# The plain first product in step 2 of a fused pooled-attention and MLP kernel, with the next query transpose and V load issued a step earlier

## The chip, the cores and the metric

One core of a Trainium2 chip runs the whole kernel. The metric is the device time of one execution in microseconds (us). The kernel before takes 282.59 us, the median of three runs (282.27 to 282.88). The profile is one execution with a span of 280.3 us.

## The reference

Two stages are fused. The first is attention over pooled keys and values: 8 batches, 8 heads, 576 queries of 64 elements; keys and values are averaged over groups of 8 rows, so each query sees 72 of them. The second is a two-layer MLP with a tanh GELU on the 4608 tokens.

```python
# q, k, v: [8, 8, 576, 64] f32;  w_in: [512, 2048], w_out: [2048, 512] f32
k_p = k.reshape(B, H, Sp, 8, D).mean(axis=3)       # Sp = 72
v_p = v.reshape(B, H, Sp, 8, D).mean(axis=3)
scores = np.matmul(q, k_p.transpose(0, 1, 3, 2)) / np.sqrt(D)
attn = softmax(scores)                             # over the 72 pooled keys
x = np.matmul(attn, v_p)                           # then heads side by side: [4608, 512]
h = x @ w_in                                       # first product
g = gelu_tanh(h)
out = g @ w_out                                    # second product, [4608, 512] f32
```

## The kernel before

The kernel works in nine steps of 512 tokens. Steps 0 to 6 and 8 are the first 512 tokens of one batch each, step 7 the 64 left over from each of the eight. During the MLP of one step, the attention of the next one is prepared: its query transpose, K pooling, K transpose, K spread, V pooling, V spread, scores, exponentials, normalisation, transposes of the weights (eT), and the V product, whose result xT the next MLP reads. Each of these is hung as a hook on a position in the row of matmuls. Positions 0 to 63 are the first product, 64 to 175 the second; a hook only says where in each engine's order an instruction stands.

The first product has two forms. The plain one has 64 matmuls of 512 columns; its outputs lie in a ring of four PSUM banks ("mm"):

```python
def hidden_two(g, hook):
    hp = [psum.tile([128, MAIN], F32, name="mm", tag="mm", bufs=4) for _ in range(2)]
    for s, (f, ko) in enumerate([(0, 0), (0, 1), (1, 0), (1, 1), (0, 2), (0, 3), (1, 2), (1, 3)]):
        hook(s)
        nc.tensor.matmul(out=hp[f], lhsT=w_in_b[:, ko, f * 128:(f + 1) * 128], rhs=st[g]["xT"][:, ko, :],
                         start=(ko == 0), stop=(ko == 3))
    for f in range(2):
        nc.scalar.activation(out=gT[:, f, :], in_=hp[f], func=ACT.Gelu_apprx_tanh)
# then 14 times hidden(): 4 matmuls of 512 columns and a GELU
```

The split one replaces half of the first product by seven products of half-sized blocks in place of eight, with sums ahead of them and additions behind, on VectorE and ScalarE. It starts in the two-bank tiles ("sc") that also hold the scores:

```python
def hidden_fast(g, hook, rest):
    y, x = [psum.tile([128, 2, MAIN], F32, name="c2", tag="sc", bufs=2) for _ in range(2)]
    # ...
    product(x4, 1, A(0, 0), X(0, 0), 0)        # 8 matmuls of 256 columns
    rest()                                     # values(g, 1): half 1 of the V product
    (t1, t2, t3, t4), make = x_sums(g)         # four VectorE sums of xT
    make(1, 2)
    k2, k0, k1 = part(), part(), spare
    nc.scalar.copy(out=k2, in_=x4)
    product(y4, 1, A(1, 0), X(1, 0), 4)
    add(out=k2, in0=y4, in1=k2, op=ALU.add)    # VectorE
    make(3, 4)
    hidden(g, 0, hook, 8)
    hidden(g, 1, hook, 12)
    product(x4, 0, S(2), T(t2), 16)
    nc.scalar.copy(out=k0, in_=x4)
    gelu(0, 0, k2)
    product(y4, 1, S(1), T(t1), 20)
    nc.vector.tensor_copy(out=k1, in_=y4)
    # ... three more products, two more additions, six more hidden()
```

The second product is split in all of the steps from 1 on. Its accumulators y, x and z are three banks of the ring of four:

```python
for n, (prod, acc, fresh) in enumerate([(1, xs, 1), (2, y, 1), (6, xs, 0), (5, z, 1), (7, xs, 0), (3, z, 0), (4, xs, 0)]):
    # 16 matmuls of 256 columns each, at positions 64 + 16 * n ...
    # after 1 and 6: ScalarE copies x out; after 5: ScalarE copies z, VectorE adds y;
    # after 7: VectorE adds x; after 3: VectorE adds z, first store;
    # after 4: ScalarE copies x, second store
```

It reads sums of the GELU's outputs (`g_sums`: per group of rows three sums on VectorE, and a fourth), the second of which overwrites a part of gT in place.

The V product has two halves of 256 tokens. Half 0 goes to an "sc" tile and one ScalarE copy takes it to xT; half 1 goes to two banks of the "mm" ring, and ScalarE and VectorE copy one each:

```python
def values(g, half, split=True):
    # half 0: one tile of tag "sc"; half 1: two tiles of tag "mm"
    # 16 matmuls of 256 columns on parts of the array (line 337)
    if half == 0 or not split:
        copy([nc.scalar, nc.vector][half], xT[:, :, t0:t0 + 256], xo)
    else:
        for i, eng in enumerate((nc.scalar, nc.vector)):
            copy(eng, xT[:, 2 * i:2 * i + 2, t0:t0 + 256], xo[i])
```

The exponentials of a step's four score tiles are ScalarE instructions that write the buffers e, of which there are three; the normalisation of tile 0 on VectorE is the last reader of its e. K and V of a step lie in one of two buffers kv, and all loads, stores and transposes of these steps are issued by one queue (SP).

Of the kernel before, what the change touches and what calls it, by code (L numbers as in the profile page):

```python
# [19 lines left out]
def kernel(  # L20
# [21 lines left out]
    nc = tc.nc  # L42
    B, H, S, D = q.shape
# [278 lines left out]
    def values(g, half, split=True):  # L322

        eT, t0 = st[g]["eT"], 256 * half
        if half == 0 or not split:
            xo = psum.tile([128, HP, 256], F32, name="xo", tag="sc", bufs=2)
            dst = [xo[:, pr, :] for pr in range(HP)]
        else:
            xo = [psum.tile([128, 2, 256], F32, name="xo", tag="mm", bufs=4) for _ in range(2)]
            dst = [xo[pr // 2][:, pr % 2, :] for pr in range(HP)]  # L330
        if g < B:
            for part, rows_ in ((SMALL, 32), (BIG, 64)):
                for pr in range(HP):
                    for hh in range(2):
                        r0, c = part[2 * pr + hh]
                        n = dict(PARTS[pr])[c]
                        nc.tensor.matmul(out=dst[pr][64 * hh:64 * hh + 64],  # L337
                                         lhsT=vbd[r0:r0 + rows_, g, n, 64 * hh:64 * hh + 64],
                                         rhs=eT[r0:r0 + rows_, 2 * half:2 * half + 2, c, :],
                                         start=(part is SMALL and pr % 2 == 0), stop=(part is BIG), skip_group_check=True)  # L340
        else:
            for pr in range(HP):
                for b in range(4):
                    p0 = 64 * (b % 2)
                    for x, (c, n) in enumerate(PARTS[pr]):
                        nc.tensor.matmul(out=dst[pr][:, 64 * b:64 * b + 64], lhsT=vbd[:, 4 * half + b, n, :],
                                         rhs=eT[:, 2 * half + b // 2, c, p0:p0 + 64], start=(x == 0), stop=(x == 1))
        xT = st[g]["xT"]
# [5 lines that stand above are left out]
# [408 lines left out]
    def at(hooks, s, f, *a):  # L762
        hooks.setdefault(s, []).append(lambda: f(*a))
# [7 lines left out]
    hooks = {}  # L771
# [46 lines left out]
    for n_, g in enumerate(seq):  # L818
        if n_ == 0:
            continue  # L820
        hooks = {}
        fast = n_ >= 2
        if n_ == 1:
            for i in range(1, 4):
                at(hooks, i, w_sums, i, 0, NP, nc.vector)
            at(hooks, 36, g_sums, 0, 4)
            at(hooks, 57, g_sums, 4, 6)
        elif fast:
            at(hooks, 41, g_sums, 0, 2, (0,))
            at(hooks, 57, g_sums, 2, 6, (0,))  # L830
            at(hooks, 65, g_sums, 6, 8, (0,))
            at(hooks, 65, g_sums, 0, 8, (1,))
        else:
            at(hooks, 20, g_sums, 0, 2)
            at(hooks, 36, g_sums, 2, 4)
            at(hooks, 57, g_sums, 4, 6)
        if not fast:
            at(hooks, 65, g_sums, 6, 8)
        if n_ + 1 < len(seq):
            n = seq[n_ + 1]  # L840
            b = B - 1 if n == R else n
            kv = n != B - 1
            if n_ == 1:
                for j in range(4):
                    at(hooks, 28 + 4 * j, cast_q, n, j, j + 1, nc.scalar)
                at(hooks, 41, qT_tile, n)
                at(hooks, 41, q_transpose_dma, n)
            if kv and not fast:
                t0 = 22 if n_ == 1 else 12
                at(hooks, t0, pool, b, 0, 5)  # L850
                at(hooks, t0, dup_k, b, 0, 5)
                at(hooks, t0, kT_tile, b, None)
                at(hooks, t0, k_transpose_dma, b)
                t1 = t0 + (16 if n_ == 1 else 24)
                at(hooks, t1, pool, b, 5, 9)
                at(hooks, t1, spread_v, b, nc.gpsimd)
                at(hooks, 56, k_spread, b, [nc.vector, nc.vector])
            elif kv:
                at(hooks, 17, pool, b, 0, 5, (1,))
                at(hooks, 17, dup_k, b, 0, 5)  # L860
                at(hooks, 17, kT_tile, b, None)
                at(hooks, 17, k_transpose_dma, b)
                if n_ == 2:
                    at(hooks, 41, pool, b, 5, 9)
                    at(hooks, 41, spread_v, b, nc.gpsimd)
                else:
                    at(hooks, 17, spread_gated, b)
                at(hooks, 40, k_spread, b, [nc.gpsimd, nc.gpsimd])
            if fast:
                at(hooks, 2, qT_tile, n)  # L870
                at(hooks, 2, q_transpose_dma, n)
                if n_ == 2:
                    at(hooks, 3, load_kv, n, (1,))
                sc_at = [76, 76, 100, 100]
                norm_at = [84, 88, 106, 106]
            else:
                sc_at = [68, 68, 94, 94]
                norm_at = [81, 97, 104, 114]
            for j in range(4):
                at(hooks, sc_at[j], scores, n, j)  # L880
                at(hooks, max(sc_at[j], 80), exps, n, j)
            at(hooks, norm_at[0], eT_tile, n)
            if fast:
                for j in (2, 3):
                    at(hooks, norm_at[j], sums, n, j)
            for j in range(4):
                at(hooks, norm_at[j], norm, n, j, nc.gpsimd if j == 1 else nc.vector)
                at(hooks, norm_at[j], e_transpose_dma, n, j)
            at(hooks, 64 + 66, nc.scalar.preload_act_table_set, GELU_SET)
            at(hooks, 64 + 100, xT_tile, n)  # L890
            at(hooks, 64 + 100, values, n, 0)
        if n_ + 2 < len(seq):
            n2 = seq[n_ + 2]
            s2 = 44 if n_ == 1 else 8 if n2 == R else 57
            at(hooks, s2, q_tile, n2)
            if n2 == R:
                at(hooks, s2, load_q, n2, 0, 2, nc.sync)
                at(hooks, 30, load_q, n2, 2, 4, nc.sync)
            else:
                at(hooks, s2, load_q, n2, 0, 4, nc.sync)  # L900
            at(hooks, 64 + 52, cast_gated, n2)
            if n2 != B - 1:
                b2 = B - 1 if n2 == R else n2
                if n_ >= 2:
                    at(hooks, 64 + 84, pool, b2, 5, 9, (0,))
                    at(hooks, 64 + 97, pool, b2, 5, 9, (1,))
                at(hooks, 64 + 98, pool, b2, 0, 5, (0,))
            if n_ == 1:
                at(hooks, 45, load_kv, n2, (0,))
            else:  # L910
                at(hooks, 28, load_kv, n2)
        mlp(g, hooks, n_ + 1 == len(seq), fast, lambda: values(g, 1))
# [30 lines left out]
```

## Time and profile before

| | |
|---|---|
| time | 282.59 us (282.27 to 282.88) |
| span of the profiled execution | 280.3 us |
| TensorE matmuls | 271.6 us busy, 97% |
| VectorE | 228.4 us busy, 81% |
| ScalarE | 176.9 us busy, 63% |
| GpSimd | 68.0 us busy, 24% |
| DMA | 54.36 MB, mean 194 GB/s |

The profile page has a row for each engine (PE is TensorE, PEld its weight loads, DVE VectorE, ACT ScalarE, POOL GpSimd), a strip of 40 slices, the chain of work that ended last, and the costliest groups of instructions by source line. The trace behind it answers more closely: a timeline (start, length, engine, line, output and inputs, and in brackets the idle time before and what ended it), a list of waits, and busy times within chosen stretches. Lines that come up below: 337 is the V product, 374 and 522 the plain first product, 465 the products of the split one, 577 the second product, 253 the exponentials, 149 to 152 the pooling of K and V, 425 to 429 the sums for the second product, 491 to 508 the copies and additions of the split first product, 449 its sums of xT, 275 the normalisation, 92 and 94 copies by ScalarE and by VectorE or GpSimd.

### The profile page before, as it was taken

What the parts mean: (1) busy time and instruction counts of PE and PEld (TensorE: products, weight loads), DVE (VectorE), ACT (ScalarE), POOL (GpSimd) and SP (SyncE); (2) the same over time, 40 slices, a digit from 0 to 9 for tenths busy, and PEclk for the clock granted to TensorE, in tenths of its full rate; (3) what the DMA queues carried; (4) which work ended last, traced back from release to release, by engine and by line L of the source; (5) the groups of instructions that cost most, each with busy time, mean ns of one, the idle gap of its engine ahead of it and who ended that gap; (6) DMA issues with size and microseconds to landing.
All of it is one profiled execution on the core that took longest, in us unless ns stands there. A gap on an engine that the chain in (4) does not pass through costs nothing.

```text
span 280.3 us, 6585 instructions
## 1 busy us (share of the span) xinstructions
PE 271.6 (97%) x2710; PEld 194.0 (69%) x2710; DVE 228.4 (81%) x370; ACT 176.9 (63%) x256; POOL 68.0 (24%) x105
## 2 busy tenths in 40 slices
PE   8989999999999979999999999999999999999995
PEld 3678844446867667668766876687668966876684
DVE  5886769998969999989998999898989378937832
ACT  1586585487647943786479647964796469646820
POOL 4740263003220634131412142214221300100000
PEclk9999999999999999999999999999999999999999
DMA  7999999999969965688869958995741860163013
GB/s 233 307 194 290 372 386 220 314 315 230 237 199 240 317 202 147 154 272 263 147 163 262 263 145 197 241 247 161 165 150 27 161 137 0 26 144 78 1 40 112
DMA packets 71695, 54.36 MB, mean 194 GB/s; under 512 B 45554, under 2 KB 57842, under 8 KB 71666
## 3 DMA queue, kind: packets, MB, share of 16 engines
q1 hardware_dynamic: 69410, 51.72, 70.3%
q0 software_dynamic: 2112, 2.10, 4.7%
q8 instruction: 21, 0.34, 0.5%
q10 hardware_dynamic: 144, 0.13, 0.1%
q14 instruction: 8, 0.07, 0.1%
HBM read 36.70 MB, written 9.44 MB: 165 GB/s over the span
## 4 chain that ended last, share of the span: by engine, by line
PE 80%; DVE 13%; DMA 3%; issue 1%; ACT 0%; POOL 0%; SPq 0%; DVEq 0%; ACTq 0%; POOLq 0%
PE mm L577 29%; PE mm L374 18%; PE c L465 14%; PE mm L385 5%; PE xo L337 3%; PE x L577 2%; DVE den L260 2%; PE warm L676 2%; PE sc L244 2%; DVE eb L275 2%; DMA qT<-q_b 2%; DMA out_dram<-osb 1%; DVE kv L149 1%; PE mm L390 1%; DVE kv L151 1%
## 5 line engine op out<-in xcount | busy, mean ns | idle before, releaser
L374 PE MATMUL mm<-xT,w_in_b 128*128 128x512 bf16 x280 | 65.2, 379 | 0.0
L577 PEld LDWEIGHTS <-gT 128*128 128x128 bf16 x512 | 48.8, 98 | 9.2 <-issue 1.6
L376 ACT ACTIVATE gT<-mm 128x512 bf16<-128x512 f32 x70 | 40.0, 598 | 12.9 <-PE mm L374 12.6
L374 PEld LDWEIGHTS <-w_in_b 128*128 128x128 bf16 x280 | 27.4, 98 | 27.1
L577 PEld LDWEIGHTS <-stage 128*128 128x128 bf16 x384 | 37.0, 98 | 6.5 <-issue 1.3
L92 ACT CAST xT<-xo 128x512 bf16<-128x512 f32 (+1 forms) x17 | 13.4, 786 | 32.3 <-PE xo L337 27.4
L577 PE MATMUL mm<-tw,gT 128*128 128x256 bf16 x240 | 29.9, 273 | 0.3 <-DVE osb L562 0.3
L577 PE MATMUL mm<-tw,stage 128*128 128x256 bf16 x224 | 28.0, 273 | 1.5 <-ACT osb L92 1.2
L172 POOL TENSOR_TENSOR vbd<-kvb,vmask 128x256 bf16<-128x256 bf16 (+2 forms) x40 | 23.4, 606 | 23.1 <-DVE kvb L152 17.0
L577 PE MATMUL mm<-w_out_b,gT 128*128 128x256 bf16 x240 | 28.9, 273 | 0.0
L260 DVE TENSOR_REDUCE den<-e 128x8 f32<-128x576 f32 x36 | 26.0, 737 | 3.5 <-ACT e L253 3.5
L253 ACT ACTIVATE e<-sc 128x576 f32<-128x576 f32 x36 | 22.6, 654 | 9.6 <-PE sc L244 4.5
L92 ACT COPY osb<-mm 128x512 f32<-128x512 f32 x30 | 17.5, 586 | 16.7 <-PE mm L577 15.6
L465 PEld LDWEIGHTS <-ws 128*128 128x128 bf16 x224 | 21.9, 98 | 7.3 <-issue 0.3
L275 POOL TENSOR_TENSOR eb<-e,r 128x576 bf16<-128x576 f32 x7 | 8.0, 1149 | 70.9 <-DVE r L269 66.1
L94 POOL CAST q_b<-q_sb 128x1024 bf16<-128x1024 f32 (+1 forms) x15 | 19.7, 1337 | 19.3 <-DMA q_sb<-in_q_dram 19.3
L149 DVE TENSOR_TENSOR kv<-kv 128x1024 f32<-128x1024 f32 (+3 forms) x19 | 21.2, 1117 | 3.2 <-DMA kv<-in_k_dram 2.1
L465 PE MATMUL c<-tt,ws 128*128 128x256 bf16 x168 | 20.8, 273 | 0.1
L275 DVE TENSOR_TENSOR eb<-e,r 128x576 bf16<-128x576 f32 x25 | 19.8, 793 | 0.9
L94 DVE CAST xT<-xo 128x512 bf16<-128x512 f32 (+1 forms) x10 | 7.4, 745 | 13.1 <-PE xo L337 7.9
L465 PEld LDWEIGHTS <-w_in_b 128*128 128x128 bf16 x168 | 15.9, 98 | 3.1 <-issue 1.2
L385 PE MATMUL mm<-xT,w_in_b 128*128 128x256 bf16 x128 | 15.6, 273 | 0.1
(105 smaller groups left out, 426.2 us busy)
## 6 DMA issues: line engine op xcount, KB each, us to landing
kv<-in_k_dram SPq DMA_DIRECT2D x7, 1024.0 KB, 7.1
q_sb<-in_q_dram SPq DMA_DIRECT2D x7, 1024.0 KB, 9.9
kv<-in_v_dram SPq DMA_DIRECT2D x6, 1024.0 KB, 8.8
out_dram<-osb SPq DMA_DIRECT2D x12, 512.0 KB, 2.9
out_dram<-osb SPq DMA_DIRECT2D x11, 256.0 KB, 4.0
kv<-in_v_dram SPq DMA_DIRECT2D x4, 512.0 KB, 9.9
w_in_b<-in_moe_w_in_dram POOLq DMA_DIRECT2D x4, 512.0 KB, 6.7
w_out_s<-in_moe_w_out_dram SPq DMA_DIRECT2D x2, 1024.0 KB, 13.5
```

Of the source, the lines that this page charges most:

```text
L92: eng.copy(out=out, in_=in_)
L94: eng.tensor_copy(out=out, in_=in_)
L149: add(out=t[:, :, 0:4, :], in0=t[:, :, 0:4, :], in1=t[:, :, 4:8, :], op=ALU.add)
L172: eng.tensor_tensor(out=vbd[p0:128, b, n0:n1, :].rearrange("p (c r) (hh d) -> p c (r hh) d", c=max(m, 1), d=D), in0=kvb[p0:128, 4 + c0:4 + ...
L253: nc.scalar.activation(out=e.rearrange("p (x h) s -> p x (h s)", x=2), in_=sc[:, :, 0:4 * Sp], func=ACT.Exp, scale=1.0 / 64.0)
L260: nc.vector.reduce_sum(out=den, in_=e, axis=AX.X)
L275: eng.tensor_tensor(out=o.rearrange("p (pr hh s) -> p hh pr s", hh=2, s=Sp), in0=e.rearrange("p (hh pr) s -> p hh pr s", hh=2), in1=r.rear ...
L374: nc.tensor.matmul(out=hp, lhsT=w_in_b[:, ko, fo * 128:(fo + 1) * 128], rhs=st[g]["xT"][:, ko, :], start=(i == 0), stop=(i == KO - 1))
L376: nc.scalar.activation(out=gT[:, fo, :], in_=hp, func=ACT.Gelu_apprx_tanh)
L385: nc.tensor.matmul(out=hp[:, f, :], lhsT=w_in_b[:, ko, (fo + f) * 128:(fo + f + 1) * 128], rhs=st[g]["xT"][:, ko, c0:c0 + 256], start=(ko ...
L465: nc.tensor.matmul(out=acc[:, m, :], lhsT=lhs(i, m), rhs=rhs(i), start=bool(fresh and i == 0 and m % 2 == 0), stop=(i == 1), skip_group_ch ...
L577: nc.tensor.matmul(out=xs[p] if acc is xs else acc[:, p, :], lhsT=lt, rhs=rt, start=bool(fresh and m == 0 and (p == 0 or (last and acc is ...
```

## The change

Step 2 gets the plain first product instead of the split one; the split form stays from step 3 on. With the plain form the hooks of step 2 become those of step 1: the sums for the second product in smaller pieces (positions 20, 36, 57, 65), K pooling for step 3 in one go at 12, V pooling and V spread at 36, K spread on VectorE at 56, scores at 68 and 94, normalisation at 81, 97, 104 and 114. There is no `rest()` in the plain form, so half 1 of step 2's V product moves to the end of step 1 (position 171). Also at the end of step 1, from position 164, stand the transpose of step 3's queries and behind it the load of step 3's V, which were issued at positions 2 and 3 of step 2; the first pass of step 3's K pooling, which stood at 162, moves into step 2. The purpose is to relieve VectorE in step 2, and to have the queries and V of step 3 on their way before it begins.

```diff
@@ for n_, g in enumerate(seq):
-        fast = n_ >= 2
+        fast = n_ >= 3
@@ elif kv:                          # steps with the split form
                 at(hooks, 17, k_transpose_dma, b)
-                if n_ == 2:
-                    at(hooks, 41, pool, b, 5, 9)
-                    at(hooks, 41, spread_v, b, nc.gpsimd)
-                else:
-                    at(hooks, 17, spread_gated, b)
+                at(hooks, 17, spread_gated, b)
                 at(hooks, 40, k_spread, b, [nc.gpsimd, nc.gpsimd])
             if fast:
                 at(hooks, 2, qT_tile, n)
                 at(hooks, 2, q_transpose_dma, n)
-                if n_ == 2:
-                    at(hooks, 3, load_kv, n, (1,))
@@
             at(hooks, 64 + 100, values, n, 0)
+            if n_ < 2:
+                at(hooks, 64 + 107, values, n, 1)
@@
             at(hooks, 64 + 52, cast_gated, n2)
-            if n2 != B - 1:
+            if n_ < 2:
+                at(hooks, 64 + 100, qT_tile, n2)
+                at(hooks, 64 + 100, q_transpose_dma, n2)
+                at(hooks, 64 + 100, load_kv, n2, (1,))
+            elif n2 != B - 1:
                 b2 = B - 1 if n2 == R else n2
-                if n_ >= 2:
-                    at(hooks, 64 + 84, pool, b2, 5, 9, (0,))
-                    at(hooks, 64 + 97, pool, b2, 5, 9, (1,))
+                at(hooks, 64 + 84, pool, b2, 5, 9, (0,))
+                at(hooks, 64 + 97, pool, b2, 5, 9, (1,))
                 at(hooks, 64 + 98, pool, b2, 0, 5, (0,))
```

On TensorE step 2 loses 56 matmuls of 256 columns and gains 32 of 512. VectorE and ScalarE lose the copies, sums and additions of one split first product, and ScalarE has 16 GELUs of 512 elements in place of eight of 512 and four of 1024.

## The prediction

> **What bounds the kernel now.** I read the page's first two blocks first: the PE row (TensorE's matmuls) is busy 97% of the 280.3 us span, the clock row is full throughout. So the whole change can only be worth the few microseconds in which TensorE waits, plus or minus the matmuls that it adds. Then I cut the trace into steps, each from the first V product of one step (line 337) to that of the next. The columns of this view are the stretch, its length, and the busy time and count of each engine; the third row here is step 4, which I take as the undisturbed pattern:
>
> ```profile
> 78.64:108.78 30.14, 28.32 (x297) 20.39 (x296) 26.73 (x41) 18.83 (x26) 8.86 (x12) 1.00 0.83 227
> 108.78:136.72 27.94, 27.94 (x297) 20.46 (x296) 26.02 (x42) 19.24 (x26) 8.57 (x13) 1.00 0.79 209
> 136.72:164.56 27.84, 27.84 (x297) 20.52 (x297) 25.30 (x41) 19.04 (x26) 7.84 (x13) 1.00 0.81 214
> ```
>
> Step 2, the first row, is 30.14 - 27.84 = 2.30 us longer than step 4 with the same matmuls: 1.82 us of idle TensorE (30.14 - 28.32), and 0.48 us that the busy column hides, because matmuls take about 0.16 us to flow again after a wait (twelve products from 99.38 should, at step 4's 1.32 us and with the 0.36 us idle shown below, end at 101.06; the next one starts at 101.23). The timeline of TensorE (start, length, then in brackets the idle before and its releaser) puts this at three places in the second product:
>
> ```profile
> 100.13 1.26 PE L577 MATMUL mm<-tw,stage 128*128 128x256 bf16 x10 [0.36 <-DVE stage L427]
> 104.31 1.91 PE L577 MATMUL mm<-tw,stage 128*128 128x256 bf16 x16 [1.17 <-ACT osb L92]
> 108.26 0.60 PE L577 MATMUL mm<-tw,gT 128*128 128x256 bf16 x4 [0.29 <-DVE osb L562]
> ```
>
> The middle one names ScalarE's copy out of PSUM, yet ScalarE was not busy. Its timeline, and VectorE's, tell why:
>
> ```profile
> 103.14 0.65 ACT L253 ACTIVATE e<-sc 128x576 f32<-128x576 f32 x1 [3.11 <-PE mm L577]
> 103.68 1.07 ACT L92 COPY osb<-mm 128x512 f32<-128x512 f32 x2
> ...
> 92.81 1.44 DVE L149 TENSOR_TENSOR kv<-kv 128x1024 f32<-128x1024 f32 x1
> ...
> 102.26 0.76 DVE L275 TENSOR_TENSOR eb<-e,r 128x576 bf16<-128x576 f32 x1
> ```
>
> The fourth exponential stood at the head of ScalarE's queue for 3.11 us. The bracket names a matmul that had long been done; the true releaser is found in the buffers. It writes one of three e buffers, and the one it needs is freed by VectorE's first normalisation, which ends at 102.26 + 0.76 = 103.02. The copy stands behind it. So all three waits have one cause: **VectorE is late in step 2.** The chain that ended last agrees: from 90.35 to 108.2 us it runs through VectorE almost alone, whereas in steps 3 to 6 it runs through TensorE. VectorE is late because only step 2 has the whole V pooling (92.81 to 95.63, 2.8 us) between the sums of the second product; later steps do it at the end of the step before.
>
> **What the Trainium skill says.** "TensorE: Matmul & The Clock Gate", section "Wait — 56ns, not 53.3ns?", gives for back-to-back matmuls N columns at 2.4 GHz plus about 2.5 ns, 215.7 ns at 512 columns. The trace agrees: 64 products of 512 columns in step 1 run from 52.22 to 66.04, 13.82 us or 215.9 ns each. The same page, under "Architectural detail", calls ScalarE and VectorE strict FIFO; the copy held behind the blocked exponential is that. "GPSIMD Engine Reference", section "1. Specifications", says that GpSimd shares its SBUF interfaces with VectorE where VectorE has two SBUF inputs. The trace agrees: the sum at line 426 takes 1.03 us at 96.27, beside GpSimd's spread of V, and 0.69 us at 60.19 without it.
>
> **The change, part by part.**
>
> 1. *Matmuls.* The split first product has 56 matmuls of 256 columns and 32 of 512. In step 2 it runs from 80.66 to 94.48, 13.82 us, with 16 V products of 0.70 us inside: 13.12. The plain one has 64 of 512, 13.82 as in step 1. So TensorE gets **+0.70 us** of work. The 16 V products are moved into step 1, not removed.
>
> 2. *VectorE.* Gone are three combining additions (1.23, 1.22, 1.23), one copy (1.21) and four sums of x (0.41, 0.42, 0.41, 0.42): 6.55 us. The K spread comes over from GpSimd: two copies, 0.93 us at 64.57 in step 1. Net -5.6 us inside the step. The first K pooling pass (1.48) moves from before the step's start to just after. None of this is on the path by itself; it is what empties the VectorE queue before the second product.
>
> 3. *The start of step 2, a new wait.* The split form starts in the wide score banks and has work while xT is copied. The plain form starts in the four-bank ring. From the last V product of step 1 at 78.64: 0.70 for half 0 of V, 7 of the remaining products 0.77, half 1 of V 0.70 (to 80.81), 5 products, and by 1.32 + 1.40 in sum TensorE is at 81.36; I add 0.1 for a second change of tile shape: 81.45. The first plain product needs xT's second half and a ring bank: the ring holds y, x, z of step 1's output, then the two V accumulators, so the next bank is x, which ScalarE copies out only after step 1's last product. ScalarE: first xT copy 79.47 to 80.48 (as now), second from 80.97 (0.58) to 81.55, copy of x 0.20 behind the last product as now (80.66 to 80.86), so 81.65 to 82.23. With 0.1 us to start, TensorE resumes at 82.33: **+0.88 us** idle that was not there.
>
> 4. *Second product of step 2.* The hooks become those of step 1, whose second product, from 66.04 to 78.64, took 12.60 us with one wait in it, 0.35 us idle plus 0.16, for the query transpose of step 2. In the new step 2 that transpose is issued a step early, so 12.60 - 0.51 = 12.09.
>
> 5. *Sum.* 82.33 + 13.82 + 12.09 = 108.24, against 108.78 now: **-0.54 us**. In other terms: -2.30 of waits, +0.70 plain product, +0.88 start, +0.1 tile change, +0.1 the looser second product. Step 3 is 0.10 longer than step 4 now, half of which may go: -0.6 in all. Steps 4 to 8 are the same instructions. 282.59 - 0.6 = **282.0 us**.
>
> *Is VectorE in time?* Its queue after the xT copy (81.66): K pooling 1.48 + 0.82 + 0.49 + 0.26 to 84.7; first sums when the fourth GELU is out (about 86.5) to 88.2; the next two from about 90.0 to 91.7; V pooling 2.33 (as at 62.25 in step 1) to 94.0; K spread to 95.0; sums 4 to 6 at step 1's slowed 2.3 to 97.3; the last, 1.7, to 99.0. TensorE reads the changed gT of the last pair at 96.15 + 1.75 + 0.39 + 0.66 = 98.95; that operand is the second of four sums, ready near 98.2. Margin 0.75.
>
> **The rivals.**
>
> A. *V lands late and VectorE stands still instead.* V of step 3 is issued behind the query transpose, which holds the issuing queue 3.28 us. Now: issue 85.26, landing 6.6 us later at 91.9. After: the transpose follows the store that issues at 79.03 (0.7), so 79.7 to 83.0, V at 83.0 + 6.6 = 89.6. Needed at 91.7. A V of 9.4 us, as another one in this stretch took, would land at 92.4, and 0.7 late is within the margin. Likely harmless; if not, 282.5 to 283.5.
>
> B. *The start is worse than 0.88.* Half 1 of V needs the last transpose of eT: issued 77.11, landed 2.6 later at 79.71; it is needed at 80.11. Now it has 1.9 us, then 0.4. If it or the copies slip by 0.6, the gain is gone: 282.6.
>
> C. *TensorE simply pays for the extra columns* and step 2's waits remain in part, because score banks and the e buffers still tie ScalarE to VectorE. For it: step 1's x addition ends at 77.71, only 0.4 us ahead of the product that needs it at 78.11. Against it: step 1 shows no such wait. It would make 282.5 to 283.3.
>
> D. *A larger gain*: the copy of x goes earlier, or the early transpose and V unload step 3 too. Down to 281.2.
>
> **Range and chances.** The gain is a difference of 2.30 and about 1.8, each known to perhaps 0.4, and the runs themselves spread by 0.6 us. I put 8 in 10 on 281.1 to 282.9. Two per cent is 5.7 us, more than twice all that is idle in step 2; only a long stall would be slower by so much.
>
> **What would show it.** Right: a wait of 0.8 to 1.0 us at line 522 for ScalarE; no wait over 0.2 us in step 2's second product, and ScalarE's fourth exponential no longer held 3 us; step 2 at about 29.6 us from V product to V product; step 3 at 27.84 to 27.94. Wrong: VectorE idle at the V pooling waiting for the V transfer (A), TensorE waiting at line 337 for eT (B), or the 1.17 us wait for the ScalarE copy still there (C).

## The result, and the profile after

The changed kernel takes 280.73 us (median of four runs, 280.68 to 280.84) against 282.50 for the kernel before: ratio 0.9937, 95% interval 0.9919 to 0.9954. Run once more beside the last experiment it took 281.09 (280.68 to 281.73), ratio 0.9956 (0.9943 to 0.9969). The gain is thus 1.2 to 1.8 us; the prediction had 0.6 and a range that ended at 281.1. The direction and the cause were right, the size was not.

The steps first, from V product to V product: this is the view of busy times in chosen stretches, for the changed kernel (stretch, length, then TensorE, weight loads, VectorE, ScalarE and GpSimd busy; the last three columns are the granted clock, the share of the DMA engines and GB/s).

```profile
78.69:107.68 28.99, 28.98 (x274) 18.26 (x274) 22.68 (x41) 18.34 (x28) 6.28 (x10) 1.00 1.00 240
107.68:135.51 27.83, 27.83 (x297) 20.49 (x297) 25.59 (x42) 19.04 (x26) 8.12 (x13) 1.00 0.80 207
135.51:163.34 27.83, 27.83 (x297) 20.51 (x296) 25.30 (x41) 19.03 (x26) 7.83 (x13) 1.00 0.81 207
```

Step 2 went from 30.14 to 28.99 us, and 28.98 of it is busy by this column. Step 3 is now as short as step 4. What TensorE does at the start of step 2, where a new wait of 0.88 us was foretold, is in its timeline, and beside it ScalarE's:

```profile
80.26 0.77 PE L337 MATMUL xo<-eT,vbd 32*64 32x256 bf16 x16
80.96 0.72 PE L577 MATMUL mm<-tw,gT 128*128 128x256 bf16 x5
81.69 1.89 PE L522 MATMUL mm<-xT,w_in_b 128*128 128x512 bf16 x8
...
81.06 0.58 ACT L92 CAST xT<-xo 128x512 bf16<-128x512 f32 x1 [0.52 <-PE xo L337]
81.72 0.59 ACT L92 COPY osb<-mm 128x512 f32<-128x512 f32 x1
```

No row of TensorE has a bracket. The plain first product (line 522) starts at 81.69, just after the copy of xT ends (81.06 + 0.58), and before ScalarE has even begun to copy x out (81.72). So it does not lie in x's bank.

In the second product, VectorE now waits for others and TensorE no longer for it; ScalarE's fourth exponential, held 3.11 us before, is held 0.56:

```profile
97.81 0.42 DVE L429 TENSOR_TENSOR stage<-gT,stage 128x512 bf16<-128x512 bf16 x1
99.11 0.75 DVE L260 TENSOR_REDUCE den<-e 128x8 f32<-128x576 f32 x1 [0.87 <-ACT e L253]
...
101.01 0.65 ACT L253 ACTIVATE e<-sc 128x576 f32<-128x576 f32 x1 [0.56 <-DVE eb L275]
```

VectorE has finished the sums at 98.2 and is idle 0.87 us before the first normalisation.

### The profile page after: what moved, and what is told of

The parts are those of the page before. It is cut to its first block, busy times and chain, and to the rows that moved or that the text cites. A ratio compares the mean times of both kernels' runs of the same rounds, so it can differ in the third digit from the quotient of the medians.

```text
span 278.8 us, 6535 instructions
## 1 busy us (share of the span) xinstructions
PE 271.8 (97%) x2686; PEld 191.8 (69%) x2686; DVE 224.3 (80%) x370; ACT 176.3 (63%) x258; POOL 64.7 (23%) x103
## 4 chain that ended last, share of the span: by engine, by line
PE 87%; DVE 7%; DMA 4%; SPq 1%; issue 0%; POOL 0%
PE mm L577 33%; PE mm L374 22%; PE c L465 13%; PE mm L385 5%; PE xo L337 3%; PE x L577 3%; PE sc L244 2%; DMA q_sb<-in_q_dram 2%; DMA qT<-q_b 2%; DVE den L260 1%; PE mm L522 1%; DVE eb L275 1%; PE mm L390 1%; DVE kv L149 1%; DVE eb L287 1%; PE xo L346 1%
## 5 line engine op out<-in xcount | busy, mean ns | idle before, releaser
L374 PE MATMUL mm<-xT,w_in_b 128*128 128x512 bf16 x304 | 69.9, 379 | 0.0
L376 ACT ACTIVATE gT<-mm 128x512 bf16<-128x512 f32 x76 | 43.9, 598 | 15.3 <-PE mm L374 14.9
L374 PEld LDWEIGHTS <-w_in_b 128*128 128x128 bf16 x304 | 29.7, 98 | 30.7
L172 POOL TENSOR_TENSOR vbd<-kvb,vmask 128x256 bf16<-128x256 bf16 (+2 forms) x40 | 22.2, 578 | 36.4 <-DVE kvb L152 27.4
L465 PEld LDWEIGHTS <-ws 128*128 128x128 bf16 x192 | 18.8, 98 | 6.0
L465 PE MATMUL c<-tt,ws 128*128 128x256 bf16 x144 | 17.7, 273 | 0.0
L425 DVE TENSOR_TENSOR stage<-gT 128x512 bf16<-128x512 bf16 (+1 forms) x25 | 13.1, 526 | 3.4 <-ACT gT L481 1.9
```

Source lines behind the costliest of these rows:

```text
L172: eng.tensor_tensor(out=vbd[p0:128, b, n0:n1, :].rearrange("p (c r) (hh d) -> p c (r hh) d", c=max(m, 1), d=D), in0=kvb[p0:128, 4 + c0:4 + ...
L374: nc.tensor.matmul(out=hp, lhsT=w_in_b[:, ko, fo * 128:(fo + 1) * 128], rhs=st[g]["xT"][:, ko, :], start=(i == 0), stop=(i == KO - 1))
L376: nc.scalar.activation(out=gT[:, fo, :], in_=hp, func=ACT.Gelu_apprx_tanh)
L465: nc.tensor.matmul(out=acc[:, m, :], lhsT=lhs(i, m), rhs=rhs(i), start=bool(fresh and i == 0 and m % 2 == 0), stop=(i == 1), skip_group_ch ...
```

## The experiments

### The first product in the bank of x

```diff
 def hidden_two(g, hook):
-    hp = [psum.tile([128, MAIN], F32, name="mm", tag="mm", bufs=4) for _ in range(2)]
+    hp = [psum.tile([128, MAIN], F32, name="mm", tag="mm", bufs=4) for _ in range(1 if g == 2 else 2)]
+    if g == 2:
+        hp.insert(0, st[1]["x"].rearrange("p a b -> p (a b)"))   # step 1's x, kept in mlp()
```

> The changed kernel, with one thing altered: the first plain product of step 2 is made to lie in the PSUM bank of x, the bank that the prediction assumed. Theory 1 (the wait of 0.88 us at the start of step 2 was missing only because the first product was given the bank of z, which is free early): TensorE now waits 0.6 to 0.9 us at the start of step 2 for ScalarE's copy of x (in the changed kernel's trace 81.72 to 82.31, against the first product's start at 81.69), and the time is 0.5 to 0.9 us above the changed kernel's 280.73, so 281.2 to 281.6. Rival 1 (the copy of x hides anyway, whatever the bank): no wait over 0.2 us, 280.6 to 280.9.

Measured: 281.53 us (280.94 to 281.84). The waits of TensorE in this kernel (waiter, releaser, total, times, longest) contain the foretold one, on the line that is 522 in the changed kernel, and its timeline shows where:

```profile
PE mm L524 <- ACT osb L92: 0.7, 1, 0.7
...
81.08 0.72 PE L579 MATMUL mm<-tw,gT 128*128 128x256 bf16 x5
82.47 1.89 PE L524 MATMUL mm<-xT,w_in_b 128*128 128x512 bf16 x8 [0.67 <-ACT osb L92]
```

Step 2 is 108.45 - 78.81 = 29.64 us long; the prediction's own sum was 108.24 - 78.64 = 29.60. With the bank that it assumed, the prediction of step 2 comes out within 0.04 us. The times alone would not settle it, since the changed kernel itself took 280.73 and 281.09 and the runs of this one begin at 280.94; the wait in the trace does. Rival 1 is out. In the program of the changed kernel the banks of step 1's y, x and z are 1, 2 and 0, the V accumulators get 3 and 1, and the first product gets 0 and 3. The pool handed out the banks in the order in which they were released: z's last reader is VectorE's addition behind the sixth of the seven products, which ends at 79.05 in the changed kernel's trace, x's is ScalarE's copy behind the seventh, which ends at 82.31.

### The transpose and V issued late, as before

```diff
-            if n_ < 2:
-                at(hooks, 64 + 100, qT_tile, n2)
-                at(hooks, 64 + 100, q_transpose_dma, n2)
-                at(hooks, 64 + 100, load_kv, n2, (1,))
+            # back to positions 2 and 3 of step 2
```

> The changed kernel, but the query transpose and the V load of step 3 are issued at positions 2 and 3 of step 2, as in the kernel before. Theory 2 (what counts is the VectorE work that the plain form takes away; the early issue is worth little): V lands near 91.9 in place of 89.6, VectorE reaches the V pooling at 90.7 and stands 1.2 us, and its 0.87 us of idle time before the exponentials take up most of it: 280.7 to 281.1. Rival 2 (the early issue is what the change lives on): the waits in step 2's second product come back in part, 281.8 or more.

Measured: 280.85 us (280.57 to 281.05), no wait of TensorE in steps 2 to 8. V comes late as foretold: VectorE stands 1.43 us before the V pooling, has no idle time left before the normalisation, and ScalarE's fourth exponential is held 1.11 us, but none of this becomes a wait of TensorE. Step 2 of this profile is 107.72 - 78.56 = 29.16 us long, 0.17 more than in the changed kernel. Theory 2 holds: with the plain product the early issue is worth nothing that the times show.

### The split product, with the early issue

```diff
 # the kernel before
-                if n_ == 2:
-                    at(hooks, 3, load_kv, n, (1,))     # and the transpose at 2
+            if n_ == 1:
+                at(hooks, 64 + 100, qT_tile, n2)
+                at(hooks, 64 + 100, q_transpose_dma, n2)
+                at(hooks, 64 + 100, load_kv, n2, (1,))
```

> The kernel before, with the split first product kept in step 2, but with the query transpose and V load of step 3 issued at the end of step 1 as in the changed kernel. Theory 2: VectorE was not waiting for V (no idle ahead of the V pooling in the trace of before), so nothing is gained: 282.2 to 282.8, with the wait of about 1.2 us for ScalarE still there. Rival 2: 281.0 to 281.6.

Measured: 288.77 us (288.53 to 289.97), which neither side expected. Three timelines of this kernel: TensorE's largest wait, ScalarE's behind it, and the issuing queue.

```profile
86.65 1.03 PE L374 MATMUL mm<-xT,w_in_b 128*128 128x512 bf16 x4
93.22 1.86 PE L465 MATMUL c<-tt,ws 128*128 128x256 bf16 x8 [5.55 <-ACT osb L498]
94.89 1.91 PE L374 MATMUL mm<-xT,w_in_b 128*128 128x512 bf16 x4
...
92.16 1.01 ACT L498 COPY osb<-c 128x1024 f32<-128x1024 f32 x1 [6.46 <-DMA out_dram<-osb]
...
79.47 3.32 SPq L228 DMA_TRANSPOSE qT<-q_b  x1
82.84 0.57 SPq L112 DMA_DIRECT2D kv<-in_v_dram  x1
83.50 0.49 SPq L406 DMA_DIRECT2D out_dram<-osb  x1
```

The second store of step 1 now stands behind the transpose and V, and lands 8.6 us after its issue at 83.50 (3.0 in the kernel before). The split product keeps its partial sums in the same two osb buffers, so ScalarE's copy at line 498 waits 6.46 us for that store, and TensorE for the copy. The stop has a second price: in this profile the granted clock reads 0.5 from 92.3 to 99.2 us, and four products of 512 columns take 1.91 us behind the wait where they took 1.03 ahead of it. From 93.22 to 99.16 TensorE works at half its rate, about 3 us lost on top of the wait. In the changed kernel the store is as slow (issued 83.56, 8.8 us), but the plain product has no partial sums: nobody asks for the buffer until the second product. So the early issue is something that the plain form makes bearable, not a gain.

### The same, the store on another queue

```diff
-                store_pair(g, 1, osb[1])
+                store_pair(g, 1, osb[1], eng=nc.scalar if g == 1 else nc.sync)
```

> The kernel with the split first product and the early issue (288.77), but the second store of step 1 is issued from ScalarE's queue, so that it no longer stands behind the query transpose and the V load. Theory 4 (the 6.3 us came from that store: it landed 8.6 us after its issue, and the split product's copy of its third product writes the same buffer and waited 6.46 us for it): back to the kernel before, 282.0 to 282.9, the copy waits under 0.5 us. Rival 4 (the transpose and V load slow step 2 by their traffic, whatever the store): 285 or more.

Measured: 283.21 us (282.97 to 283.68). The store lands 5.0 us after its issue in place of 8.6, the copy's wait is 0.8 us in place of 6.46 (under 0.5 was expected), the clock stays full in step 2, and 5.6 us of the 6.3 are back: theory 4. It stays 0.7 above the kernel before, outside what was expected. Step 2 is not the reason, 30.22 us long in the profile; step 3 has a wait of 0.82 us for a transpose of eT that no other run shows there. It landed 4.2 us after its issue (2.6 in the kernel before); why is not shown.

### V pooling left out

```diff
 # the kernel before
-                    at(hooks, 41, pool, b, 5, 9)
+                    at(hooks, 41, skip_pool_v, b)   # one copy of unpooled V: step 3's output is not the reference's
```

> The kernel before, with the V pooling of step 3 left out of VectorE's work in step 2: one small copy of unpooled V stands in for three additions (2.75 us), so step 3's output is not the reference's. Theory 3 (the three waits in step 2 all come from VectorE being about 3 us late): at least 1.8 of the 2.30 us go, TensorE's wait for ScalarE is under 0.3 us, 280.2 to 280.8. Rival 3 (the waits belong to the split form itself in step 2, its score banks and e buffers): the wait for ScalarE stays above 0.8 us, 281.5 or more.

Measured: 280.25 us (280.17 to 280.44), 2.26 below the kernel before. These are all waits of TensorE from step 2 on:

```profile
PE c L468 <- DVE stage L507: 0.2, 1, 0.2
PE mm L580 <- DVE osb L565: 0.2, 1, 0.2
...
106.60 0.60 PE L580 MATMUL mm<-tw,gT 128*128 128x256 bf16 x4 [0.17 <-DVE osb L565]
```

The 1.17 us wait for ScalarE and the 0.36 us wait for the sums are gone, though only VectorE's work was touched, and step 2 is 107.12 - 78.96 = 28.16 us long in place of 30.14. Theory 3 holds for these two: one lateness made both. The third wait, for VectorE's addition (line 562 before, 565 here), only fell from 0.29 to 0.17 us. V pooling is a part of its cause and not all of it.

### V pooling on GpSimd

```diff
 # the kernel before
-                    at(hooks, 41, pool, b, 5, 9)
+                    at(hooks, 41, pool, b, 5, 9, (0, 1), nc.gpsimd)
-                at(hooks, 40, k_spread, b, [nc.gpsimd, nc.gpsimd])
+                at(hooks, 43 if n_ == 2 else 40, k_spread, b, [nc.vector, nc.vector] if n_ == 2 else [nc.gpsimd, nc.gpsimd])
```

> The kernel before, with the split product in step 2, but the V pooling of step 3 done by GpSimd instead of VectorE, and in exchange the K spread by VectorE: VectorE is relieved of 2.75 - 0.93 = 1.8 of its about 3 us lateness. Theory 3 (lateness of VectorE sets the waits, bit by bit): a part of the 2.30 us goes, 280.9 to 281.8, the wait for ScalarE between 0 and 0.8 us. Rival 3b (GpSimd's pooling slows VectorE's two-input sums beside it as much as it relieves it): 282 or more.

Measured: 284.44 us (283.74 to 285.31), slower than the kernel before: rival 3b, and more. VectorE's and GpSimd's timelines:

```profile
92.11 2.52 DVE L426 TENSOR_TENSOR gT<-gT 128x512 bf16<-128x512 bf16 x1
94.66 1.37 DVE L427 TENSOR_TENSOR stage<-gT 128x512 bf16<-128x512 bf16 x1
...
91.99 2.35 POOL L149 TENSOR_TENSOR kv<-kv 128x1024 f32<-128x1024 f32 x1 [13.17 <-DMA kv<-in_v_dram]
```

The sum at line 426 takes 2.52 us where it took 0.42 in the kernel before, for as long as GpSimd's first addition runs. Moving 2.75 us of pooling away cost VectorE 3.05 us on this and the next sum alone (2.52 + 1.37 - 0.42 - 0.42), and the K spread then came late for the scores, for which TensorE waits 0.80 us. VectorE was not relieved, so this run says nothing on theory 3.

### Two tries at the wait that is left in step 1

```diff
 # scores of step 2 at 72 in place of 68 (first run)
-                sc_at = [68, 68, 94, 94]
+                sc_at = [72, 72, 94, 94] if n_ == 1 else [68, 68, 94, 94]
 # queries of step 2 loaded ahead of K and V, cast and transposed 8 matmuls earlier (second run)
 # (the moved load, and the transpose at 33 in place of 41, are left out here)
-                    at(hooks, 28 + 4 * j, cast_q, n, j, j + 1, nc.scalar)
+                    at(hooks, 20 + 4 * j, cast_q, n, j, j + 1, nc.scalar)
```

> The changed kernel, with the first two score products of step 2 (which run in step 1) four matmuls later, at position 72 in place of 68. Theory 5 (the one wait left in the steady part, 0.35 us plus 0.16 to flow again, is for the query transpose that lands just too late, and 0.44 us of matmuls cover it): the wait is gone, 280.1 to 280.5. Rival 5 (the scores, exponentials and VectorE's chain end later by as much, and the wait comes back at the x addition): 280.6 to 280.9.

> The changed kernel, with the queries of step 2 loaded ahead of its K and V in step 0, and cast and transposed eight matmuls earlier in step 1. The wait of 0.35 us (plus 0.16) for that transpose in step 1 should go without moving the scores: 280.1 to 280.5. If instead K, now loaded behind, lands too late for VectorE's pooling at 56.1, VectorE is late in step 1 and nothing is gained: 280.6 to 281.2.

Measured: 280.67 us (280.34 to 281.15) and 280.92 (280.70 to 281.51), the second beside 281.09 for the changed kernel on the same chip. In both profiles the wait for the query transpose in step 1 is gone. In the first, 0.15 us of it comes back as a wait for eT at half 1 of V, the margin that rival B named. Both times lie above the 280.1 to 280.5 that was expected. What remains of the 0.5 us is less than these runs differ among themselves, so no version better than the changed kernel is established.

### Both kernels once more

> The kernel before, once more, for a second profile: the step lengths (27.8 us from step 4 on, 30.1 in step 2) should come out the same within 0.1 us; whether the last step again shows about 0.3 us of idle TensorE behind a store that lands late tells whether that part of the difference between the two profiles belongs to the change.

> The changed kernel once more, beside the last one on the same chip: 280.5 to 280.9, step 2 at 29.0 us and step 3 at 27.8 us from V product to V product, no wait of TensorE in steps 2 to 8.

Measured: 282.37 us (one run) and 281.09 (six runs), the latter above the 280.5 to 280.9 expected. Second profiles, the kernel before above, the changed one below:

```profile
79.00:109.15 30.15, 28.32 (x298) 20.43 (x298) 26.74 (x41) 18.84 (x26) 8.56 (x12) 1.00 0.81 229
109.15:137.39 28.24, 28.04 (x297) 20.51 (x296) 26.10 (x42) 19.16 (x26) 8.58 (x13) 1.00 0.88 206
...
78.81:107.80 28.99, 28.98 (x275) 18.27 (x274) 22.48 (x41) 18.35 (x28) 5.91 (x10) 1.00 1.05 238
107.80:135.63 27.83, 27.83 (x298) 20.50 (x298) 25.59 (x42) 19.03 (x26) 8.13 (x13) 1.00 0.81 209
```

Step 2 repeats to 0.01 us in both kernels. Step 3 repeats to 0.01 in the changed kernel (27.83), but not in the kernel before (27.94, then 28.24). The last stretch, from the V product of the last step (248.32 and 248.99 before, 247.10 and 247.22 after) to the end of the span, is 32.0 and 31.7 us before, 31.7 and 31.7 after: the 0.3 us more of the first profile of before was a store that landed late, and no part of the change.

## Why the prediction was wrong, point by point

**The bound and the cause: right in the main.** TensorE was the bound, and the waits in step 2 came from VectorE's lateness. The changed kernel shows none of the three, and leaving out V pooling alone shortens step 2 by 1.98 us and the time by 2.26. That all three waits have V pooling as their one cause is too much: of the third, 0.17 us stay without it.

**The 0.16 us behind a wait: right in size, not in cause.** The matmuls are not slow to flow again: behind the wait at 100.13 ten products take 1.10 us, 0.11 each, which is the full rate. The idle time in the bracket is counted from the end of the matmul ahead, 0.27 us after its start, whereas the next one would have started 0.11 after that start; the difference is 0.16. So a wait costs its bracket plus 0.16 us, and one shorter than 0.16 can be lost from view.

**Matmuls: right.** The plain product runs from 81.69 to 95.50, 13.81 us for 13.82.

**VectorE: right.** It loses 26.73 - 22.68 = 4.05 us of busy time in step 2; the parts gave -5.6 + 1.48 = -4.1.

**The start of step 2: the step that failed.** The prediction said "the next bank is x". The bank was z's, because the pool is not the ring that the prediction took it for. The copies were timed well (the copy of x at 81.72, foretold 81.65), but the one of x is not on the path: TensorE resumed 81.69 - 78.69 = 3.00 us after the step's start, and not 82.33 - 78.64 = 3.69. Forcing the assumed bank gave the wait back: the start came at 82.47 - 78.81 = 3.66. What was left of the foretold 0.88 us is small. The last five products of step 1 start at 80.96 and take 0.11 each, so TensorE is through at 81.51 and starts 0.18 later, 0.05 behind the end of ScalarE's copy of xT; the bracket doesn't show it. With z's bank the prediction's own figures give the same: copy of xT to 81.55, 0.1 to start, 3.01 us after the step's start. The term should have been read from the bank of each tile, not from the order in which the source asks for them.

**The second product: nearly.** 95.50 to 107.68, 12.18 us for 12.09. The other small term, the V half moved into step 1, cost what was foretold: TensorE is through with step 1 at 81.51 - 78.69 = 2.82 us, foretold 81.45 - 78.64 = 2.81.

**Step 3: sized too small.** Half of 0.10 us was foretold. VectorE's lateness goes on into step 3, by way of a store. These are VectorE, ScalarE and TensorE in the second profile of the kernel before, then VectorE and ScalarE in the changed one:

```profile
109.61 0.69 DVE L599 TENSOR_TENSOR osb<-mm,osb 128x512 f32<-128x512 f32 x1
114.05 1.01 ACT L491 COPY osb<-c 128x1024 f32<-128x1024 f32 x1 [0.53 <-DVE tt L449]
121.08 1.03 PE L465 MATMUL c<-tt,w_in_b 128*128 128x256 bf16 x8 [0.20 <-DVE stage L504]
...
107.70 0.68 DVE L599 TENSOR_TENSOR osb<-mm,osb 128x512 f32<-128x512 f32 x1
111.94 1.02 ACT L491 COPY osb<-c 128x1024 f32<-128x1024 f32 x1
```

In the kernel before, the last addition of step 2 (line 599) starts 0.46 us after the V product that opens step 3, in the changed kernel 0.02 after it. Behind it goes the first store, which lands at 113.97 and at 111.04. ScalarE's first copy of the split product writes the same buffer. In the kernel before it starts at 114.05, 0.08 behind that landing, so it waited for the store and not for the VectorE sum in the bracket. It starts 4.90 us after the V product, in the changed kernel 4.26. That its delay then runs through VectorE to TensorE's 0.20 us at line 465 is read from the order of the work, not tested. The gain is 0.11 and 0.41 us in the two profiles of before.

**The sum.** Two profiles of each kernel have spans of 280.3 and 280.7, and of 278.8 and 278.9: 1.65 us apart. Of these 1.16 are step 2, foretold 0.54, and 0.26 step 3, foretold 0.05. The bank, 0.69, is the whole of the first gap, the second product's 0.09 taking a little back. The other 0.2 lie in the first two steps and the last, which differ as much between two profiles of one kernel.

**The rivals.** A (V late) did not come, and would not have mattered: with V issued late on purpose VectorE stood 1.43 us and the time was the same. B came only when the scores were moved, 0.15 us. C did not come. D (a larger gain) came, but by neither of its ways: the copy of x was not earlier (81.72 for 81.65), and with the transpose and V issued late step 3 stays at 27.83 us.

**The range** was laid out as a spread of 0.4 us around a sum. But the start term was a question of yes or no: x's bank and a start at 82.33, or another and one at 81.65. The answer no takes 0.68 us off the 282.0, which makes 281.3, close to the lower end of the range, and the underrated step 3 and the spread of the runs then had no room. A term like this makes two humps, and the range has to hold both.

## What to carry to other kernels

Before a wait for a buffer is put into a sum, find which buffer the allocator hands out: it may be the one released first, and then a wait that looks certain is not there. Where several waits of one engine cluster in one stage, look for the one late engine behind them; here a wait put down to an idle ScalarE was VectorE's, through a buffer count and queue order. A transfer issued early also pushes back what stands behind it in its queue; ask which buffer that holds and who wants it next.

## What the runs showed of the hardware that was not expected

A 512 KB store took 8.6 and 8.8 us from issue to landing when it stood behind a query transpose and a 1024 KB load in the same queue, and 3.0 us without them; on ScalarE's queue, beside the same two, it took 5.0. When TensorE had stood 5.55 us, the granted clock read 0.5 for 6.8 us, and four products of 512 columns took 1.91 us in place of 1.03. And VectorE's bf16 sum of two tensors took 2.52 us in place of 0.42 beside a float32 addition on GpSimd that ran 2.35 us, while beside GpSimd's bf16 V spread the sum of twice the size took 1.03 in place of 0.69. That the two engines share their SBUF interfaces is what the Trainium skill says ("GPSIMD Engine Reference", section "1. Specifications"); in this run VectorE all but stopped for the length of one GpSimd instruction.
